# P times V of a sliding-window attention in eight 64x32 array tiles, with the halves added on GpSimd and the transposed maxima four slots later

## The chip, the core and the metric

The kernel runs on one core of a Trainium2 chip. A core has five engines with a queue each, which take their instructions in order and meet through semaphores: TensorE (PE in the profile, its weight loads PEld), VectorE (DVE), ScalarE (ACT), GpSimd (POOL) and SyncE (SP), which here only issues DMAs. TensorE multiplies out of SBUF into PSUM, which has eight banks of 128 partitions by 512 fp32 values. The metric is the device time of one execution in microseconds (us).

## The reference

The output is x + attention(LN(x)) + GEGLU(LN(x)) for 2048 tokens of width 640, all in fp32. What the change touches is the attention: 32 heads of width 20, each query seeing itself and the 255 keys before it.

```python
B, S, D = x.shape                       # 1, 2048, 640
H = 32; Dh = D // H; W = 256
qkv = (x @ wqkv) ...                    # q, k, v: heads of width 20
scores = jnp.einsum("bhqd,bhkd->bhqk", q, k) * (Dh ** -0.5)
mask = (idx[:, None] - idx[None, :] >= 0) & (idx[:, None] - idx[None, :] < W)
p = _softmax(jnp.where(mask, scores, -1e9), axis=-1)
o = jnp.einsum("bhqk,bhkd->bhqd", p, v)
# o @ wo is added to x and to (gelu(xn @ w_gate) * (xn @ w_up)) @ w_down
```

## The kernel before

The attention is cut into 32 units, one for each group `g` of four heads and each chunk `c` of 512 queries (`u = 4 * g + c`). It is run between about 90 and 575 us of the span in an order written out by hand: a loop over units, each of 14 slots, that says in every slot which instructions each engine gets next. Into each slot it also puts some 2.4 dense matmuls (128x512) of other work, the q, k and v projections and the first gate and up tiles, so that TensorE always has something to do (`pull_fill`, line 110).

A unit passes through these steps, the first two of them ahead of its own slots.

- `max_pair` (line 522): bf16 scores of 64 queries by up to 320 keys for the row maxima, in 64x64 tiles of the array, two PSUM banks for a pair. VectorE reduces each bank with a mask (line 526, into `junk` and `mx`). Two pairs are issued as a burst at slots 0, 4 and 8, and at slot 0 two more behind the P times V product. The order behind that product is: four banks of maxima, then the first score of the next unit.
- `max_end` (lines 543 to 546): the negated maxima `nm` are transposed by TensorE into `ps_n`, copied by ScalarE to `mr` and sent by a DMA from ScalarE's queue into two extra rows of the query stack `qs`, so that the score matmul subtracts the maximum. `MXD` sets how many slots after the last maxima this happens: 6, which is slot 6, eight slots ahead of the unit's first score.
- `exp_piece` (lines 581 and 583): for s = 0 to 11 a bank of scores, transposed (keys in the partitions), then exp on ScalarE into a tile `P`. Four of them, one for each head, share a `P` tile; three `P` tiles X, Z and Y (s = 0 to 3, 4 to 7, 8 to 11) hold the unit's key blocks. s = 0 is in slot 0, 1 to 4 in slot 2, 5 and 6 in slot 4, 7 and 8 in slot 8, 9 to 11 in slot 10.
- `clear` (lines 594 and 597): GpSimd zeroes, one slot after the last exp of a `P` tile, what lies outside the window, 128 keys by 128 queries of four heads at a time. For Y those are three instructions, the last of them for key block b+3.
- `av_unit` (lines 608 and 612): at slot 0 of the next unit, V (128 keys by 20 columns and a column of ones, 32 columns of the array for each head) times P. Four heads run beside each other in four 128x32 tiles, six key blocks one after the other in the order X, Z, Y, 1536 columns in all (four blocks and 1152 columns for c = 0). All goes into one bank `ps_o`; ScalarE copies it to `ob`, and SyncE stores it three slots later.

The banks `ps_m`, `ps_n`, `ps_e` and `ps_o` come out of one pool of six (`psr`, tag `ring`); the other two hold the dense tiles. A tile of the pool may be written once its last reader is done, and TensorE, which takes its queue in order, waits at the first matmul into it.

```python
BURSTS = 0, 4, 8
SCORES = {0: range(0, 1), 2: range(1, 5), 4: range(5, 7), 8: range(7, 9), 10: range(9, 12)}
MXD = 6
psr = pp.enter_context(tc.tile_pool(name="psr", bufs=6, space=PSUM, reuse_waits="tile"))
```

Of the kernel before, what the change touches and what calls it, by code (L numbers as in the profile page):

```python
# [9 lines left out]
F32 = mybir.dt.float32  # L10
F32R = mybir.dt.float32r
BF = mybir.dt.bfloat16
AF = mybir.ActivationFunctionType
OP = mybir.AluOpType
# [5 lines left out]
C = 512  # L20
# [15 lines left out]
VEARLY = 2  # L36
VLEAD = 40
POOL_SLOTS = 13, 0, 1, 2, 3, 4, 5, 6, 7
MXD = 6
KSLOT = 9  # L40
LAG = 3, 5, 4, 4, 4, 4, 3, 3, 4, 3, 2, 1, 1, 1
NFA = 4
# [28 lines left out]
def block_kernel(ctx, tc, x, wqk, wv, wgu, wdo, wdl, out):  # L71
    nc = tc.nc
# [120 lines left out]
    done = set()  # L193
    now = [None]

    def at(slot, fn, *a):
        acts.setdefault(slot, []).append((fn, a))
# [31 lines left out]
    def defer(n, fn, *a):  # L229
        if now[0] is None:  # L230
            fn(*a)
        else:
            at(now[0] + n, fn, *a)
# [190 lines left out]
    with tc.tile_pool(name="lp", bufs=1, side="right") as lp:  # L424
# [5 lines left out]
        ps = psd.tile([128, C], F32, name="ps_u", tag="dn")  # L430
# [48 lines left out]
    vtiles = dict(enumerate(v0[2]))  # L479
    pf.close()  # L480
    psr = pp.enter_context(tc.tile_pool(name="psr", bufs=6, space=PSUM, reuse_waits="tile"))
    ap = pr.enter_context(tc.tile_pool(name="ap", bufs=2, side="right", reuse_waits="tile"))
# [14 lines left out]
    def bank(name):  # L497
        return psr.tile([128, C], F32, name=name, tag="ring")
# [49 lines left out]
    def pieces(c):  # L548
        b = 4 * c
        X = [(b, 0, 0, 384)] + ([(b - 2, 384, 0, 128)] if c else [])  # L550
        Y = [(b + 1, 0, 128, 384), (b + 3, 384, 384, 128)]
        Z = ([(b - 1, 0, 0, 256)] if c else []) + [(b + 2, 256, 256, 256)]
        return X, Z, Y
# [11 lines left out]
    pts = {}  # L565
# [21 lines left out]
    def clear(u, bi):  # L587
        c = u % NC
        pt = pts[u, bi]
        for p in pieces(c)[bi]:  # L590
            for col, diag in diag_tail(*p, c):
# [4 lines left out]
                else:  # L596
                    nc.gpsimd.affine_select(out=a, in_=a, pattern=[[0, 4], [-1, 128]], compare_op=OP.is_ge,  # L597
                                            fill=0.0, base=-1, channel_multiplier=1)

    def av_unit(u):  # L600
        g, c = divmod(u, NC)
        o, v = bank("ps_o"), vtiles[g]
        todo = [(pts[u, bi], *p) for bi, ps in enumerate(pieces(c)) for p in ps]
        for i, (pt, kb, col, q0, n) in enumerate(todo):
            assert (id(v), kb) in done, (u, kb)
            for j in range(4):
                w0_ = kb * 84 + 21 * j
                nc.tensor.matmul(o[32 * j:32 * j + 32, q0:q0 + n], v[:, w0_:w0_ + 32], pt[:, j, col:col + n],  # L608
                                 start=i == 0, stop=i == len(todo) - 1, skip_group_check=True,
                                 tile_position=(0, 32 * j))  # L610
        ob = ap.tile([128, C], F32, name="ob", tag="ob", bufs=1)
        nc.scalar.activation(ob, o, AF.Copy)  # L612

        def store():
            for j in range(4):
                nc.sync.dma_start(od[c].rearrange("(d h) t -> h d t", h=H)[4 * g + j], ob[32 * j:32 * j + DH, :])
            nc.sync.dma_start(sd[c][4 * g:4 * g + 4, :], ob[DH::32, :])

        defer(3, store)

    def load_gu(f):
        raws = []
# [163 lines left out]
    def pull_max(n, slot):  # L786
        for _ in range(n):
# [4 lines left out]
            if x[1] == 7:  # L792
                at(slot + (MXD if slot >= 0 else 4), max_end, x[0])

# [9 lines left out]
    def attention():  # L804
# [18 lines left out]
        for u in range(NU + 1):  # L823
            for i in range(NS):
                T = now[0] = NS * u + i
                for fn, a in tick():
                    fn(*a)
                if i in BURSTS:
                    pull_max(2, T)
                if i == 0 and u:  # L830
                    av_unit(u - 1)
                    flush()
                    pull_max(2, T)
                for s in SCORES.get(i, ()) if u < NU else ():
# [673 lines left out]
```

## Time and profile before

| what | value |
|---|---|
| time, median of 3 runs | 1047.59 us (1047.58 to 1047.95) |
| span of the profiled execution | 1046.8 us, about 0.8 us less than the median of the runs |
| granted TensorE clock, mean | 0.999 |
| TensorE matmul busy | 1035.2 us, 99% of the span |
| VectorE, ScalarE, GpSimd busy | 70%, 49%, 32% of the span |
| P times V (line 608) | 1408 matmul records, 84.3 us busy |
| copy of it (line 612) | 32, 597 ns each |

An fp32 matmul of the program stands in the trace as two weight loads and two matmul records. Records carry modelled ends that reach past the start of the next matmul, so what a group costs TensorE is read from its start to the start of what follows. Times in the rows are from the span's start; `[0.33 <-ACT ob L612]` is idle time before the row and what ended it.

### The profile page before, as it was taken

How to read it: one execution, taken by the hardware profiler on the slowest of the kernel's cores; microseconds unless marked ns; L12 is line 12 of the kernel's file. 1: busy time of each engine (PE TensorE's matmuls, PEld its weight loads, DVE VectorE, ACT ScalarE, POOL GpSimd, SP SyncE). 2: the span in 40 equal slices, each digit the busy share in tenths (PEclk: the TensorE clock that was granted, in tenths of full speed). 3: DMA queues.
4: the chain of work that ended last, by engine and by line, in shares of the span. 5: the costliest groups of instructions: out<-in, count | busy, mean ns of one | idle time of the engine just before them, and what ended most of it. 6: DMA issues, size and time to landing. Idle time of an engine off the chain costs nothing.

```text
span 1046.8 us, 22733 instructions
## 1 busy us (share of the span) xinstructions
PE 1035.2 (99%) x7997; PEld 827.6 (79%) x7997; DVE 730.8 (70%) x2007; ACT 513.5 (49%) x1088; POOL 333.8 (32%) x503
## 2 busy tenths in 40 slices
PE   8999999999999999999999999999999999999998
PEld 7987666666677766666666888888888999999998
DVE  8745656666665556677662677877655889888887
ACT  4444666765665566656565532223324554333332
POOL 5122667766464458474635111110110000000000
PEclk9999999999999999999999999999999999999999
DMA  5651465545332344444322557677217874443342
GB/s 200 189 150 59 135 183 159 179 148 180 96 117 72 111 145 144 139 130 130 112 79 75 191 189 244 213 251 253 100 61 250 270 241 137 134 128 113 125 134 94
DMA packets 105179, 158.56 MB, mean 151 GB/s; under 512 B 15420, under 2 KB 60092, under 8 KB 105064
## 3 DMA queue, kind: packets, MB, share of 16 engines
q1 hardware_dynamic: 102680, 150.95, 45.0%
q10 hardware_dynamic: 2384, 6.16, 1.9%
q8 instruction: 63, 1.03, 0.4%
q14 instruction: 52, 0.43, 0.1%
HBM read 101.78 MB, written 54.92 MB: 150 GB/s over the span
## 4 chain that ended last, share of the span: by engine, by line
PE 92%; DVE 3%; DMA 2%; ACT 1%; POOL 1%; issue 1%; SPq 0%; DVEq 0%; POOLq 0%; ACTq 0%
PE ps_g L952 21%; PE ps L1219 21%; PE ps_d L110 21%; PE ps_e L581 8%; PE ps_o L608 7%; PE ps_v L110 7%; PE ps_m L522 4%; PE ps_g L110 1%; PE ps_t L181 1%; DVE junk L526 1%; DMA qs<-qd 1%; PE ps_d L356 1%; DVE ss L1057 0%; POOL pt L259 0%; DVE at L1057 0%
## 5 line engine op out<-in xcount | busy, mean ns | idle before, releaser
L526 DVE CUSTOM_DVE_ANT_0 junk<-ps_m,mask 128x320 bf16<-128x320 f32 (+2 forms) x512 | 243.2, 475 | 144.5 <-PE ps_m L522 85.5
L583 ACT ACTIVATE P<-ps_e 128x512 f32<-128x512 f32 (+2 forms) x384 | 195.6, 578 | 60.9 <-PE ps_e L581 59.0
L1219 PE MATMUL ps<-wb,at 128*128 128x320 f32 x999 | 156.0, 309 | 0.0
L1219 PEld LDWEIGHTS ps<-wb,at 128*128 128x128 f32 x999 | 148.9, 188 | 0.3
L594 POOL TENSOR_SCALAR_AFFINE_SELECT P<-P 128x512 f32<-128x512 f32 x128 | 83.9, 657 | 141.0 <-ACT P L583 138.3
L581 PE MATMUL ps_e<-qs,ks 124*128 124x128 bf16 (+2 forms) x704 | 108.0, 277 | 0.7 <-DVE mx L526 0.4
L110 PE MATMUL ps_d<-xh,wqh 128*128 128x512 f32 x350 | 104.4, 410 | 0.0
L110 PE MATMUL ps_d<-xl,wqh 128*128 128x512 f32 x350 | 104.2, 409 | 0.0
L110 PE MATMUL ps_d<-xh,wql 128*128 128x512 f32 x350 | 103.8, 409 | 0.0
L1219 PE MATMUL ps<-wt,at 128*128 128x320 f32 x552 | 89.2, 309 | 0.4 <-DVE u L1057 0.4
L581 PEld LDWEIGHTS <-ks 124*128 124x128 bf16 x704 | 50.8, 98 | 47.8 <-issue 30.1
L608 PE MATMUL ps_o<-P,v 128*32 128x384 f32 (+2 forms) x1408 | 84.3, 386 | 0.6 <-DVE mx L526 0.6
L1219 PEld LDWEIGHTS ps<-wt,at 128*128 128x128 f32 x552 | 82.9, 188 | 0.9 <-DVE u L1057 0.9
L597 POOL TENSOR_SCALAR_AFFINE_SELECT P<-P 128x512 f32<-128x512 f32 x112 | 70.8, 643 | 33.7 <-ACT P L583 33.7
L1173 ACT ACTIVATE at<-ss 128x512 fp32r<-128x512 f32 x59 | 37.3, 632 | 89.6 <-DVE ss L1057 89.6
L103 POOL TENSOR_TENSOR wql<-wr,wqh 128x640 fp32r<-128x640 f32 x11 | 17.6, 1607 | 174.0 <-PE ps_g L952 129.4
L110 PEld LDWEIGHTS ps_d<-xh,wql 128*128 128x128 f32 x350 | 63.9, 189 | 11.1 <-issue 0.3
L608 PEld LDWEIGHTS ps_o<-P,v 128*32 128x32 f32 x1408 | 41.5, 110 | 39.0 <-issue 21.1
L110 PEld LDWEIGHTS ps_d<-xl,wqh 128*128 128x128 f32 x350 | 63.8, 189 | 10.5 <-issue 0.2
L110 PEld LDWEIGHTS ps_d<-xh,wqh 128*128 128x128 f32 x350 | 63.4, 189 | 10.7 <-issue 0.3
L259 POOL TENSOR_TENSOR pt<-r,pt 128x512 bf16<-128x512 f32 x40 | 46.8, 1170 | 67.3 <-ACT pt L258 67.2
L612 ACT ACTIVATE ob<-ps_o 128x512 f32<-128x512 f32 x32 | 19.1, 597 | 86.6 <-PE ps_o L608 72.3
(194 smaller groups left out, 1846.0 us busy)
## 6 DMA issues: line engine op xcount, KB each, us to landing
hr<-hd SPq DMA_DIRECT2D x104, 128.0 KB
hd<-he SPq DMA_DIRECT2D x50, 256.0 KB
wr<-wgu SPq DMA_DIRECT2D x27, 320.0 KB
qs<-qd SPq DMA_DIRECT2D x64, 120.0 KB
ks<-kd SPq DMA_DIRECT2D x64, 120.0 KB
xi<-x SPq DMA_DIRECT2D x16, 320.0 KB
qs<-qd SPq DMA_DIRECT2D x64, 80.0 KB
ks<-kd SPq DMA_DIRECT2D x64, 80.0 KB
```

The costliest lines, as they stand in the source:

```text
L110: nc.tensor.matmul(ps, a(k), b(k), start=n == 0, stop=n == 3 * nk - 1)
L259: nc.gpsimd.tensor_tensor(out=pt[:, l, :], in0=r, in1=pt[:, 1, :], op=OP.subtract)
L522: nc.tensor.matmul(ps[64 * h:64 * h + 64, lo:hi], q[rows, j, q0:q0 + 64], keys, start=True, stop=True, tile_position=(64 * r, 64 * h))
L526: nc.vector.tensor_tensor_reduce(out=junk[:, 0:n], in0=ps[:, 0:n], in1=mask[:, 320 - n:320], scale=1.0, scalar=NEG, op0=OP.add, op1=OP.max ...
L581: nc.tensor.matmul(ps[:, col:col + n], k[0:QROWS, j, kc:kc + 128], q[0:QROWS, j, q0:q0 + n], start=True, stop=True)
L583: nc.scalar.activation(pt[:, j, lo:hi], ps[:, lo:hi], AF.Exp, scale=SCALE)
L594: nc.gpsimd.affine_select(out=a, in_=a, pattern=[[0, 4], [1, 128]], compare_op=OP.is_ge, fill=0.0, base=0, channel_multiplier=-1)
L597: nc.gpsimd.affine_select(out=a, in_=a, pattern=[[0, 4], [-1, 128]], compare_op=OP.is_ge, fill=0.0, base=-1, channel_multiplier=1)
L608: nc.tensor.matmul(o[32 * j:32 * j + 32, q0:q0 + n], v[:, w0_:w0_ + 32], pt[:, j, col:col + n], start=i == 0, stop=i == len(todo) - 1, ski ...
L952: nc.tensor.matmul(ps, i, j, start=first and n == 0, stop=n == len(work) - 1, skip_group_check=True)
L1173: nc.scalar.activation(hi[:, 3:7], s, AF.Copy)
L1219: nc.tensor.matmul(ps[bank][:, 0:HD], *work[bank][j], start=bank not in begun, stop=final[p, bank] == n and j == len(work[bank]) - 1, skip ...
```

## The change

It has three parts.

1. The product is split by keys: each block of 128 keys becomes two halves of 64, which use the upper and the lower 64 rows of the array, so that eight 64x32 tiles (two halves by four heads) take part. Each half of a block meets only the queries of its own window, at most 320 columns (384 where c = 0 and the first key block fills the columns ahead of it). Halves of equal width are paired, in a new order: for c > 0 first key block b+0 with itself, then half 0 of b+3 with half 1 of b-2, and so on, with b+1 last. Each half has a bank of its own, so a unit takes two banks `ps_o` instead of one.
2. ScalarE copies both banks, the second into the first quarter of the unit's `P` tile Y (`other`), and one slot later GpSimd adds the two (new line 630). The store comes a slot later, in the fourth.
3. `MXD` is 10: the transpose of the negated maxima stands at the head of slot 10, ahead of the scores s = 9 to 11, and its DMA behind their exps.

```diff
-MXD = 6
+MXD = 10
...
+    def windows(c):
+        r = {}
+        for bi, ps in enumerate(pieces(c)):
+            for kb, col, q0, n in ps:
+                for h in range(2):
+                    first = 128 * (kb - 4 * c) + 64 * h
+                    lo = max(0, first) if kb else 0
+                    hi = min(C, first + 320)
+                    r[h, kb - 4 * c] = bi, kb, col + lo - q0, lo, hi - lo
+        pairs = [((0, 0), (1, 0)), ((0, 3), (1, -2)), ((0, -2), (1, 3)), ((0, 2), (1, -1)), ((0, -1), (1, 2)),
+                 ((0, 1), (1, 1))]
+        if not c:
+            pairs = [((0, d), (1, d)) for d in range(4)]
+        return [[(h, *r[h, d]) for h, d in p] for p in pairs]
...
-        o, v = bank("ps_o"), vtiles[g]
-        todo = [(pts[u, bi], *p) for bi, ps in enumerate(pieces(c)) for p in ps]
...
+        halves, v = [bank("ps_o") for _ in range(2)], vtiles[g]
+        todo = windows(c)
+        for i, pair in enumerate(todo):
             for j in range(4):
...
+                for h, bi, kb, col, q0, n in pair:
+                    rows, w0_ = slice(64 * h, 64 * h + 64), kb * 84 + 21 * j
+                    nc.tensor.matmul(halves[h][32 * j:32 * j + 32, q0:q0 + n], v[rows, w0_:w0_ + 32],
+                                     pts[u, bi][rows, j, col:col + n], start=i == 0, stop=i == len(todo) - 1,
+                                     skip_group_check=True, tile_position=(64 * h, 32 * j))
+        ob, other = ap.tile([128, C], F32, name="ob", tag="ob", bufs=1), pts[u, 2][:, 0, :]
+        nc.scalar.activation(ob, halves[0], AF.Copy)
+        nc.scalar.activation(other, halves[1], AF.Copy)
+        defer(1, lambda: nc.gpsimd.tensor_tensor(out=ob, in0=ob, in1=other, op=OP.add))
...
-        defer(3, store)
+        defer(4, store)
```

How the instructions stand is shown at three places, all of the unit u = 10 (c = 2); a name in brackets says whose semaphore an instruction waits for. The first is TensorE's product, before: X (384 and 128 columns), Z (twice 256), Y (384 and 128), each with its own wait for GpSimd's clears.

```order
L608 MATMUL ps_o<-P,v 32x384 [waits Activation_49,Pool_49]
L608 MATMUL ps_o<-P,v 32x384 x3
L608 MATMUL ps_o<-P,v 32x128 [waits Pool_49]
L608 MATMUL ps_o<-P,v 32x128 x3
L608 MATMUL ps_o<-P,v 32x256 [waits Pool_49]
L608 MATMUL ps_o<-P,v 32x256 x3
L608 MATMUL ps_o<-P,v 32x256 [waits Pool_49]
L608 MATMUL ps_o<-P,v 32x256 x3
L608 MATMUL ps_o<-P,v 32x384 [waits Pool_49]
L608 MATMUL ps_o<-P,v 32x384 x2
L608 MATMUL ps_o<-P,v 32x384 [waits Activation_49]
L608 MATMUL ps_o<-P,v 32x128 [waits Pool_49]
```

The same product with the change (line 624), eight matmuls for each pair of halves:

```order
L624 MATMUL ps_o<-P,v 32x320 [waits Activation_49,Pool_49]
L624 MATMUL ps_o<-P,v 32x320 [waits Activation_49]
L624 MATMUL ps_o<-P,v 32x320 x6
L624 MATMUL ps_o<-P,v 32x128 [waits Pool_49]
L624 MATMUL ps_o<-P,v 32x128 x7
L624 MATMUL ps_o<-P,v 32x64 x8
L624 MATMUL ps_o<-P,v 32x256 x8
L624 MATMUL ps_o<-P,v 32x192 x8
L624 MATMUL ps_o<-P,v 32x320 x8
```

The last wait for GpSimd, for key block b+3 out of Y, has moved from behind five blocks to behind the first pair.

The second place is on TensorE too: the end of the burst behind the product and the next unit's first score (`ps_e`, line 581), before,

```order
L522 LDWEIGHTS qs_166
L522 MATMUL ps_m<-ks_169,qs_166 64x320
L581 LDWEIGHTS ks_171 [waits DMAHW6_49]
L581 MATMUL ps_e<-qs_168,ks_171 128x128 [waits DVE_49]
L581 LDWEIGHTS ks_172
L581 MATMUL ps_e<-qs_168,ks_172 128x384
L110 MATMUL ps_d<-xh_77,wql 128x512
```

and with the change:

```order
L522 LDWEIGHTS qs_166
L522 MATMUL ps_m<-ks_169,qs_166 64x320
L581 LDWEIGHTS ks_171 [waits DMAHW3_49,DMAHW0_49]
L581 MATMUL ps_e<-qs_168,ks_171 128x128 [waits Activation_49]
L581 LDWEIGHTS ks_172
L581 MATMUL ps_e<-qs_168,ks_172 128x384
L110 MATMUL ps_d<-xh_77,wql 128x512
```

The first score's bank is freed by a reduction of VectorE before and by ScalarE with the change: in the built program it is the bank of the product's first half, in 29 of the 30 units that have a second burst (in the other, u = 9, the burst's last bank is that one).

The third place is ScalarE's queue from slot 8 to the copy of the next product, before,

```order
L545 ACTIVATE mr<-ps_n 32x128 [waits PE_49]
L546 DMA qs_168<-mr 2x16x128 [waits DMAHW6_49,Activation_49]
L583 ACTIVATE P<-ps_e 128x512 [waits PE_49]
L583 ACTIVATE P<-ps_e 128x512 [waits PE_49,Pool_49]
L665 ACTIVATE he<-he 128x512 [waits DVE_49]
L583 ACTIVATE P<-ps_e 128x512 [waits PE_49] x3
L612 ACTIVATE ob<-ps_o 128x512 [waits DMAHW2_49,DMAHW5_49,DMAHW1_49,DMAHW7_49,DMAHW0_49,PE_49]
```

and with the change:

```order
L583 ACTIVATE P<-ps_e 128x512 [waits PE_49]
L583 ACTIVATE P<-ps_e 128x512 [waits PE_49,Pool_49]
L683 ACTIVATE he<-he 128x512 [waits DVE_49]
L545 ACTIVATE mr<-ps_n 32x128 [waits PE_49]
L583 ACTIVATE P<-ps_e 128x512 [waits PE_49] x3
L546 DMA qs_168<-mr 2x16x128 [waits DMAHW3_49,Activation_49]
L628 ACTIVATE ob<-ps_o 128x512 [waits DMAHW5_49,DMAHW6_49,DMAHW1_49,DMAHW7_49,DMAHW0_49,PE_49]
L629 ACTIVATE P<-ps_o 128x512 [waits PE_49,Pool_49]
```

The copy `mr` stands ahead of the three exps of slot 10 and its DMA behind them, and a second copy follows the first.

More of the change, by code (lines that the diff above doesn't have):

```diff
@@ L600, in av_unit @@
     def av_unit(u):
         g, c = divmod(u, NC)
-        o, v = bank("ps_o"), vtiles[g]
-        todo = [(pts[u, bi], *p) for bi, ps in enumerate(pieces(c)) for p in ps]
-        for i, (pt, kb, col, q0, n) in enumerate(todo):
-            assert (id(v), kb) in done, (u, kb)
+        halves, v = [bank("ps_o") for _ in range(2)], vtiles[g]
+        todo = windows(c)
+        for i, pair in enumerate(todo):
             for j in range(4):
[L607 to L610, printed above, removed]
@@ L611, in av_unit @@
-        ob = ap.tile([128, C], F32, name="ob", tag="ob", bufs=1)
-        nc.scalar.activation(ob, o, AF.Copy)
+                for h, bi, kb, col, q0, n in pair:
+                    assert (id(v), kb) in done, (u, kb)
+                    rows, w0_ = slice(64 * h, 64 * h + 64), kb * 84 + 21 * j
+                    nc.tensor.matmul(halves[h][32 * j:32 * j + 32, q0:q0 + n], v[rows, w0_:w0_ + 32],
+                                     pts[u, bi][rows, j, col:col + n], start=i == 0, stop=i == len(todo) - 1,
+                                     skip_group_check=True, tile_position=(64 * h, 32 * j))
```

## The prediction

> **What bounds the kernel now.** I read the page first, then one row of busy times for the attention, then TensorE's order of time around two products.
>
> ```profile
> span 1046.8 us, 22733 instructions
> PE 1035.2 (99%) x7997; PEld 827.6 (79%) x7997; DVE 730.8 (70%) x2007; ACT 513.5 (49%) x1088; POOL 333.8 (32%) x503
> PE 92%; DVE 3%; DMA 2%; ACT 1%; POOL 1%; issue 1%; SPq 0%; DVEq 0%; POOLq 0%; ACTq 0%
> ...
> 90.00:575.00 485.00, 481.67 (x4756) 323.20 (x4745) 302.30 (x1120) 299.16 (x652) 280.55 (x440) 1.00 0.42 127
> ```
>
> TensorE carries 92% of the chain that ended last, and in the attention (90 to 575 us; the columns are length, then PE, PEld, DVE, ACT and POOL busy, clock, DMA share and GB/s) it has matmuls for 481.67 of 485.00 us, at full clock. The other engines are busy some 60%. So whatever shortens or stalls TensorE there moves the end one for one, and a wait of another engine costs nothing until TensorE meets it.
>
> ```profile
> 165.97 2.15 PE L608 MATMUL ps_o<-P,v 128*32 128x384 f32 x32
> 168.04 0.47 PE L522 MATMUL ps_m<-ks,qs 60*64 60x320 bf16 x8
> ...
> 240.89 2.80 PE L608 MATMUL ps_o<-P,v 128*32 128x384 f32 x48
> 243.62 0.46 PE L522 MATMUL ps_m<-ks,qs 60*64 60x320 bf16 x5
> 244.41 0.33 PE L522 MATMUL ps_m<-ks,qs 60*64 60x320 bf16 x3 [0.33 <-ACT ob L612]
> 244.67 0.39 PE L581 MATMUL ps_e<-qs,ks 124*128 124x128 bf16 x2
> ...
> 256.51 0.36 PE L522 MATMUL ps_m<-ks,qs 60*64 60x64 bf16 x12
> 256.81 2.80 PE L608 MATMUL ps_o<-P,v 128*32 128x384 f32 x48
> 259.53 0.47 PE L522 MATMUL ps_m<-ks,qs 60*64 60x320 bf16 x8
> 259.93 0.39 PE L581 MATMUL ps_e<-qs,ks 124*128 124x128 bf16 x2
> ...
> 261.08 1.05 PE L581 MATMUL ps_e<-qs,ks 124*128 124x128 bf16 x8
> ```
>
> These are three products (starts are the first column) with the burst and the first score behind them. From start to start a product costs 256.81 to 259.53 = 2.72 us, or 2.07 for c = 0 (165.97 to 168.04). At 240.89 the burst stops halfway for the copy `ob`: that will be the model for the change.
>
> **The product.** The two lengths differ by 384 columns and 0.65 us, so a column costs 1.69 ns and 2.72 - 1536 x 1.69 ns leaves 0.12 us for start and drain. If all eight tiles run at once, a unit has 1280 columns instead of 1536: 256 x 1.69 ns = 0.43 us less. For c = 0 the longer half has 1024 instead of 1152: 0.22 us less. Sum: 24 x 0.433 + 8 x 0.217 = 12.1 us gained. Do the two row halves run at once? No fp32 row shows it, but the maxima do so in bf16: their eight matmuls of 320 columns in four 64x64 tiles take 0.40 us (259.53 to 259.93), 0.05 each, drain included, where the dense stage pays 0.156 for one of 320:
>
> ```profile
> L1219 PE MATMUL ps<-wb,at 128*128 128x320 f32 x999 | 156.0, 309 | 0.0
> ...
> 256.81 0.53 PE L608 MATMUL ps_o<-P,v 128*32 128x384 f32 x4
> ```
>
> The second row, asked for the 50 ns up to 256.84, shows four fp32 column tiles started within 0.03 us. I take the full 12.1; the other end, halves in turn, is a rival.
>
> **The first score's wait.** The product's two banks leave four of the six for the bursts, and the first score takes the first half's bank, which the first copy has to empty.
>
> ```profile
> 243.76 0.60 ACT L612 ACTIVATE ob<-ps_o 128x512 f32<-128x512 f32 x1 [1.46 <-PE ps_o L608]
> ...
> 259.67 0.60 ACT L612 ACTIVATE ob<-ps_o 128x512 f32<-128x512 f32 x1 [4.20 <-PE ps_o L608]
> ...
> L522 PE MATMUL ps_m<-ks,qs 60*64 60x320 bf16 x512 | 30.5, 308 | 0.7 <-ACT ob L612 0.7
> ```
>
> ScalarE stands idle when the product ends, so the copy starts 0.14 us behind it (259.67 - 259.53), takes 0.60, and TensorE resumes 0.05 later (243.76 + 0.60 to 244.41): 0.79 us behind the product, where the score now comes at 0.40 (259.93). That is +0.39 us for a unit. The last row holds before's whole price for it: two units whose burst meets that bank, 0.33 idle each, and whose score comes 1.05 us behind the product (244.67 - 243.62). In one of the two it will be 0.79; in another one the burst's last bank is still the product's, so 1.05 stays. Sum: 28 x 0.39 - 0.26 = 10.7 us lost. The second copy costs TensorE nothing: it ends 0.14 + 2 x 0.60 = 1.34 us behind the product at the latest, and its bank is next used in slot 2, which begins 1.15 us behind the first score (259.93 to 261.08), so at 1.94. So nearly all of the product's gain goes back here. In the Trainium skill, "TensorEngine Tiling (Array Packing)", section Performance Considerations, PSUM Bottleneck, says that tiling speeds up TensorE but not the emptying of PSUM, so that the copy can become the bottleneck; the wait at 244.41 agrees.
>
> **The clears.** For c > 0 the second pair needs the last clear of Y; before, Y came behind X and Z. The first pair ends 0.02 + 320 x 1.69 ns = 0.56 us into the product. To see what GpSimd still has to do then, I asked for the work on `P` from 0.51 us (0.05 for the semaphore, as above) to 2.60 us into each of the 24 products:
>
> ```profile
> 119.96:122.05 2.09, 2.09 (x47) 1.13 (x36) 0.00 (x0) 0.00 (x0) 1.00 0.61 199
> 135.00:137.09 2.09, 2.09 (x47) 1.08 (x36) 0.00 (x0) 1.69 (x3) 1.00 0.78 243
> ...
> 568.50:570.59 2.09, 2.09 (x47) 1.13 (x36) 0.00 (x0) 0.73 (x2) 1.00 0.05 22
> sum 50.18, PE 50.18 PEld 27.04 ACT 0.00 POOL 9.38; mean PE 2.09 PEld 1.13 ACT 0.00 POOL 0.39
> ```
>
> The fourth busy time is POOL: nothing in the first stretch, 1.69 us in the worst, 9.38 in all (the first two, the last, and the sum of the 24). The clears run back to back there, so this is what TensorE would wait: 9.4 us lost, ahead of the copy, so it adds to the wait above. For c = 0 the second pair needs only earlier clears, and I put it at nothing.
>
> **The add.** GpSimd gets 32 additions of 128x512 fp32, which no row shows. The nearest are
>
> ```profile
> L259 POOL TENSOR_TENSOR pt<-r,pt 128x512 bf16<-128x512 f32 x40 | 46.8, 1170 | 67.3 <-ACT pt L258 67.2 <-DMA ks<-kd 0.2
> L739 POOL TENSOR_TENSOR tx<-tx,xl 128x256 f32<-128x256 f32 x48 | 36.2, 754 | 1.7
> ...
> 182.00:194.00 12.00, 11.20 (x18) 1.00 0.57 173
> 391.60:403.00 11.40, 11.12 (x18) 1.00 0.36 112
> ```
>
> so 1.17 to 1.51 us (twice 0.754). Behind it on the queue stand the clears. In most units GpSimd idles for microseconds before these; in the two stretches shown (POOL busy is the number behind the length) only 0.80 and 0.28 us are left, so 1.5 us more delays the clears by 0.7 and 1.2. I take 1.9 us lost, between nothing and 7.5 (five such units, 1.5 each). The store, one slot later behind the add, is followed by SyncE's other transfers, which are needed a unit later: nothing.
>
> **The moved transpose.** The matmul is the same, and its bank is free earlier than the scores'. ScalarE gets `mr` (0.26) ahead of three exps and 0.62 us of DMA issue behind them:
>
> ```profile
> 250.10 0.23 PE L543 MATMUL ps_n<-identb,nm 128*128 128x128 bf16 x1
> ...
> 250.84 0.26 ACT L545 ACTIVATE mr<-ps_n 32x128 bf16<-32x128 f32 x1
> 251.13 0.65 ACTq L546 DMA_DIRECT2D qs<-mr  x1
> ...
> 253.90 1.57 ACT L583 ACTIVATE P<-ps_e 128x512 f32<-128x512 f32 x3
> ```
>
> Here the exps would end at 255.47 and the issue at 256.12; the score that reads the row came at 259.93 and would come no more than 0.43 sooner: 3.4 us for a transfer of 8 KB. Nothing, with that as cover.
>
> **Sum.** -12.1 + 10.7 + 9.4 + 1.9 = +9.9 us on the execution's 1046.8, and 0.8 more to the median: 1057.5 us, 0.9% slower.
>
> **Rivals.**
> - The clears don't bind, because GpSimd comes earlier in the new order: -12.1 + 10.7 = -1.4, 1046.2 us, no change. Against it: nothing that feeds the clears is moved ahead.
> - Faster: the first score waits for an older reader of ScalarE's and not for the copy. Then the score comes at 0.40 again, before's two long waits go too (-1.3), and the sum is -12.1 - 1.3 + 9.4 + 1.9 = -2.1, or -4.0 if the add hides: 1044.5. It decides from a wait under 0.2 us on. Against it: the bank is the first half's.
> - The short matmuls are bound by their starts. Twelve of the maxima take 0.30 us (256.51 to 256.81), 25 ns each; 96 records at 25 ns and 0.12 make a product 2.52 us, which gains 0.20 instead of 0.43 in 24 units: 5.6 us more than my sum, 1063. Against it: the four starts within 0.03 us. The Trainium skill, "TensorE: Matmul & The Clock Gate", Part 1 (Wait — 56ns, not 53.3ns?), has this as a rule, no start closer than about 25 ns to the last; the four starts disagree.
> - The halves take turns in fp32: 2560 columns, 24 x 1.73 + 8 x 1.41 = 53 us lost instead of 12 gained; Y then waits less, some 2.5: 53 + 10.7 + 2.5, 1114 us.
> - The maxima come late: a landing 1 us past the 3.4 would cost 31 units 1 us each, 1088.
>
> **How the numbers follow.** What a measurement can tell from no change is about 0.2%, 2.1 us. The forecast has 0.66, with a range of its own of 1051 to 1062 (the add's two ends, and the waits a quarter off); clears that don't bind 0.07 (same); the older reader 0.06 and both together 0.04 (faster, 1034 to 1045); bound starts 0.07, halves in turn 0.06, late maxima 0.04 (all slower). So faster 0.10, same 0.07, slower 0.83. The range takes in forecast, bound starts and the clears' case, 0.80: 1046 to 1064.
>
> **What would show it.** In the profile after, a product with no wait for GpSimd in it costs 2.29 us (c > 0); line 581 or 522 idles behind ACT's copy of `ps_o` in every unit but two, with the score 0.79 us behind the product; and line 624 idles behind POOL at the second pair, 0.2 us in many units and over 1 in a few. A product of 4.4 us would show halves in turn, 2.5 bound starts, and a wait for a DMA at line 581 late maxima. The forecast is wrong if GpSimd's clears move against the product, since the 9.4 us come from their place in the trace of before.

## The result, and the profile after

The changed kernel takes 1063.95 us (median; 1063.40 to 1064.86), the kernel before beside it 1047.77 us: 1.0152 times as long, with a 95% interval of 1.0138 to 1.0167. It is slower, by 16 us. The profiled execution has a span of 1062.1 us, 15.3 more than before.

From the profile after: the page's span, busy times and chain of waits, then the row of busy times for the attention (90 to 586 us; length, then PE, PEld, DVE, ACT and POOL busy, clock, DMA share, GB/s).

```profile
span 1062.1 us, 25620 instructions
PE 1035.2 (97%) x9405; PEld 842.0 (79%) x9405; DVE 738.5 (70%) x2007; ACT 526.9 (50%) x1120; POOL 373.6 (35%) x535
PE 78%; DVE 6%; ACT 5%; POOL 4%; DMA 4%; issue 2%; SPq 1%; DVEq 0%; ACTq 0%; POOLq 0%
...
90.00:586.00 496.00, 476.71 (x6147) 333.63 (x6135) 305.94 (x1115) 311.78 (x681) 317.69 (x470) 1.00 0.42 124
```

TensorE is busy for the same 1035.2 us as before; by the page the whole difference is time in which it has nothing running. (Busy time counts the records' modelled ends, which reach into the waits; by starts the products did get 7.5 us shorter, as the table below shows.) Its share of the chain fell from 92% to 78%, and the rest went to ScalarE, GpSimd, VectorE and DMA. The clock is full in both.

Next the groups of lines 581 (scores) and 624 (the product, line 608 before), and TensorE's order of time: an undisturbed product (unit 21; units count the products from 0), the worst one (unit 2), and the last.

```profile
L581 PE MATMUL ps_e<-qs,ks 124*128 124x128 bf16 (+2 forms) x704 | 107.1, 276 | 7.8 <-ACT ob L628 6.1 <-DVE mx L526 1.5
L624 PE MATMUL ps_o<-P,v 64*32 64x320 f32 (+5 forms) x2816 | 81.8, 351 | 7.4 <-POOL P L594 5.8 <-POOL P L597 1.1 <-DVE mx L526 0.4
```

```profile
135.81 0.77 PE L624 MATMUL ps_o<-P,v 64*32 64x320 f32 x16
138.15 2.01 PE L624 MATMUL ps_o<-P,v 64*32 64x128 f32 x80 [1.57 <-POOL P L594]
140.09 0.47 PE L522 MATMUL ps_m<-ks,qs 60*64 60x320 bf16 x8
140.83 0.38 PE L581 MATMUL ps_e<-qs,ks 124*128 124x128 bf16 x2 [0.27 <-ACT ob L628]
...
429.20 2.55 PE L624 MATMUL ps_o<-P,v 64*32 64x320 f32 x96
431.69 0.47 PE L522 MATMUL ps_m<-ks,qs 60*64 60x320 bf16 x8
432.42 0.38 PE L581 MATMUL ps_e<-qs,ks 124*128 124x128 bf16 x2 [0.27 <-ACT ob L628]
...
583.02 2.01 PE L624 MATMUL ps_o<-P,v 64*32 64x128 f32 x80 [0.53 <-POOL P L594]
584.97 0.73 PE L110 MATMUL ps_d<-xl,wqh 128*128 128x512 f32 x2
586.19 0.96 PE L110 MATMUL ps_g<-xh,wqh 128*128 128x512 f32 x3 [0.49 <-ACT P L629]
```

Three things are to be seen. A product that waits for nothing takes 2.48 us (429.20 to 431.69), where it took 2.73. Behind it the first score waits for ScalarE's copy of the first half, 0.74 us behind the product instead of 0.40. And at unit 2 the second pair of 128 columns waits for GpSimd's clears: the product takes 4.28 us. The last row is new too: the dense stage behind the last product stops for the second copy.

I split the execution at three starts in each unit: the product's first record, the burst's first record behind it, and the first score. Summed over the units, against before:

| stretch | change, us |
|---|---|
| before the first product | +0.6 |
| products, without waits for GpSimd (24 x 0.245 and 8 x 0.197 shorter) | -7.5 |
| waits for GpSimd inside products, c > 0 | +9.9 |
| the same, c = 0 (units 0 and 24) | +2.1 |
| product to first score | +9.9 |
| first score to next product | -0.8 |
| behind the last product | about +1.1 |
| span | +15.3 |

A wait for GpSimd is what a product lasts over 2.48 us (c > 0) or 1.88 us (c = 0). It is more than the 7.4 us of idle time at line 624, because the modelled end of the matmul before covers the first 0.2 to 0.3 us of each wait (at unit 2 the row shows 1.57 us, and by starts it is 1.80).

### The profile page after: what moved, and what is told of

It reads as the page before. It is cut to its first block, busy times and chain, and to the rows that moved or that the text cites. A ratio compares the mean times of both kernels' runs of the same rounds, so it can differ in the third digit from the quotient of the medians.

```text
span 1062.1 us, 25620 instructions
## 1 busy us (share of the span) xinstructions
PE 1035.2 (97%) x9405; PEld 842.0 (79%) x9405; DVE 738.5 (70%) x2007; ACT 526.9 (50%) x1120; POOL 373.6 (35%) x535
## 4 chain that ended last, share of the span: by engine, by line
PE 78%; DVE 6%; ACT 5%; POOL 4%; DMA 4%; issue 2%; SPq 1%; DVEq 0%; ACTq 0%; POOLq 0%
PE ps_g L970 20%; PE ps L1237 18%; PE ps_d L110 17%; PE ps_e L581 6%; PE ps_v L110 6%; PE ps_o L624 6%; PE ps_m L522 3%; DVE junk L526 2%; ACT P L583 2%; POOL P L594 2%; PE ps_g L110 1%; POOL P L597 1%; ACT ob L628 1%; PE ps_t L181 1%; DVE at L1075 1%
## 5 line engine op out<-in xcount | busy, mean ns | idle before, releaser
L624 PE MATMUL ps_o<-P,v 64*32 64x320 f32 (+5 forms) x2816 | 81.8, 351 | 7.4 <-POOL P L594 5.8
L581 PEld LDWEIGHTS <-ks 124*128 124x128 bf16 x704 | 53.3, 98 | 44.9 <-issue 27.4
L110 PEld LDWEIGHTS ps_d<-xh,wqh 128*128 128x128 f32 x350 | 63.8, 189 | 11.4 <-issue 0.3
L624 PEld LDWEIGHTS ps_o<-P,v 64*32 64x32 f32 x2816 | 49.7, 105 | 27.6 <-POOL P L594 18.4
L522 PEld LDWEIGHTS <-qs 60*64 60x64 bf16 x1472 | 27.2, 105 | 51.0 <-issue 44.3
```

The lines of the kernel that those rows point to most:

```text
L110: nc.tensor.matmul(ps, a(k), b(k), start=n == 0, stop=n == 3 * nk - 1)
L522: nc.tensor.matmul(ps[64 * h:64 * h + 64, lo:hi], q[rows, j, q0:q0 + 64], keys, start=True, stop=True, tile_position=(64 * r, 64 * h))
L581: nc.tensor.matmul(ps[:, col:col + n], k[0:QROWS, j, kc:kc + 128], q[0:QROWS, j, q0:q0 + n], start=True, stop=True)
L624: nc.tensor.matmul(halves[h][32 * j:32 * j + 32, q0:q0 + n], v[rows, w0_:w0_ + 32], pts[u, bi][rows, j, col:col + n], start=i == 0, stop=i ...
```

## The experiments

Each is compared with the kernel before, run on the same chip; 1.0152 is the changed kernel's ratio. Differences between experiments are taken between these ratios, or between starts in the traces.

**Two banks for the product.** First I wanted the bank alone, without tiles:

```diff
-        o, v = bank("ps_o"), vtiles[g]
+        o, spare, v = bank("ps_o"), bank("ps_o"), vtiles[g]
```

> The kernel before, whose product now takes two banks of the ring and leaves the second one empty; nothing else differs. Theory (the first score waits because its bank is one further on in the ring, and that is the bank the copy empties): the score comes 0.74 us behind the product, as in the changed kernel, and not 0.40, in some 28 units: 28 x 0.34 - 0.3 = +9.2 us, 1057 us. Rival (the wait belongs to the two copies, or to the tiles, and not to the number of banks): the score stays at 0.40 and the time at 1047.7.

Measured: 1.0001 (0.9992 to 1.0011), and nothing in the trace moved: the score stayed at 0.40, and the same two bursts as before stopped for the copy. A tile that nothing writes evidently held no bank, so this run tells nothing about the theory. The next one fills both banks:

```diff
-        o, v = bank("ps_o"), vtiles[g]
+        halves, v = [bank("ps_o") for _ in range(2)], vtiles[g]
...
+                o = halves[int(n == 256)]
...
-        nc.scalar.activation(ob, o, AF.Copy)
+        ob, other = ap.tile([128, C], F32, name="ob", tag="ob", bufs=1), pts[u, 2][:, 0, :]
+        a = 0 if c else 256
+        nc.scalar.activation(ob, halves[0], AF.Copy)
+        nc.scalar.activation(other[:, a:C], halves[1][:, a:C], AF.Copy)
+        defer(1, lambda: nc.gpsimd.tensor_tensor(out=ob[:, a:C], in0=ob[:, a:C], in1=other[:, a:C], op=OP.add))
...
```

> The kernel before, its product still of whole blocks of 128 rows in four tiles and in the old order, but written into two banks (the pieces X and Y into one, Z into the other), both copied by ScalarE and added on GpSimd. So the changed kernel without its tiles, its order of pairs and its moved transpose. Theory (the bank is what the first score waits for): the product stays at 2.73 us, the score comes 0.74 to 0.79 us behind it and the rest of the unit gives 0.09 of that back, as in the changed kernel: 30 x 0.25 = 7.5, with 1.5 at the first and the last unit 9 us over before, 1057 us. Rival (the score's wait comes of the shorter product and its tiles): 1048 to 1050 us, the score at 0.40.

Measured: 1.0119 (1.0104 to 1.0134), 12.4 us slower. TensorE at unit 21 of this kernel, and its line of scores:

```profile
428.26 2.80 PE L609 MATMUL ps_o<-P,v 128*32 128x384 f32 x48
430.99 0.47 PE L522 MATMUL ps_m<-ks,qs 60*64 60x320 bf16 x8
431.77 0.38 PE L581 MATMUL ps_e<-qs,ks 124*128 124x128 bf16 x2 [0.32 <-ACT ob L614]
...
L581 PE MATMUL ps_e<-qs,ks 124*128 124x128 bf16 (+2 forms) x704 | 107.6, 277 | 8.3 <-ACT ob L614 6.1 <-DMA qs<-qd 0.8 <-DVE mx L526 0.4
```

The product is the old one, 2.73 us, and the score comes 0.78 to 0.79 us behind it (1.27 in the two units that had 1.05). The stretches between product and score grew by 11.3 us in all, and the rest of the units gave only 0.6 back. Another 0.8 us is a wait of unit 24's product for GpSimd, and 0.9 stand behind the last product. So the price of the second bank is paid without any tile. The theory holds, and its price of 9 us was low: this rest gives back next to nothing, where I had put 0.09 a unit.

**The first score one slot later.**

```diff
-SCORES = {0: range(0, 1), 2: range(1, 5), 4: range(5, 7), 8: range(7, 9), 10: range(9, 12)}
+SCORES = {1: range(0, 1), 2: range(1, 5), 4: range(5, 7), 8: range(7, 9), 10: range(9, 12)}
```

> The changed kernel with the unit's first score one slot later, so that two to four dense matmuls stand between the burst and this score. Theory: they cover the copy that empties the score's bank; the 9.9 us between products and first scores come back, 1064.0 - 9.9 = 1054 us, and line 581 has no idle time behind ScalarE's copy. Rival (the wait only moves: the scores of slot 2 or the exponentials behind them come as late as they did): 1064 us, with the idle time behind ScalarE at another line.

Measured: 1.0127 (1.0112 to 1.0142), 2.6 us below the changed kernel and not 9.9. TensorE at unit 21, and at a product with c = 0 (unit 28, at 538.72); then the kernel's longest kinds of wait (total, times, longest):

```profile
432.69 0.47 PE L522 MATMUL ps_m<-ks,qs 60*64 60x320 bf16 x8
433.09 0.96 PE L110 MATMUL ps_d<-xh,wqh 128*128 128x512 f32 x3
433.89 0.40 PE L581 MATMUL ps_e<-qs,ks 124*128 124x128 bf16 x2
...
538.72 1.95 PE L624 MATMUL ps_o<-P,v 64*32 64x320 f32 x64
540.60 0.91 PE L522 MATMUL ps_m<-ks,qs 60*64 60x320 bf16 x8
541.44 0.96 PE L110 MATMUL ps_d<-xh,wqh 128*128 128x512 f32 x3
...
PE ps_o L624 <- POOL P L594: 6.5, 10, 1.6
PE ps_t L181 <- DVE xi L164: 2.4, 3, 1.5
PE ps_m L522 <- DMA qs<-qd: 2.2, 3, 1.5
```

The wait for the copy is gone: in an ordinary c > 0 unit the stretch from product to next product is 0.07 us over before where the changed kernel has 0.25 (medians), so nearly 0.2 us did come back in each of 16 such units, 3.3 us together. I had expected the 0.34 at the score; the changed kernel's unit had already given 0.09 of it back, in dense work that came closer. It went again elsewhere: the wait for `qs` near 160 us grew (the rest of unit 3 is 1.4 us longer than in the changed kernel), GpSimd's clears came 0.6 us later against unit 6's product, and with c = 0 nothing was won, since there the burst itself takes 0.84 us (540.60 to 541.44) instead of 0.40, ahead of the score. That happens only behind the c = 0 product of 1.88 us in two banks; that VectorE has not yet emptied the banks of the burst before is what I take for its cause. Its rows fit (the last of those four reductions runs from 540.63 to 541.12 us), but no run here isolates it. In the profiled execution the units as a whole gave nothing back, 0.3 us more than in the changed kernel; its span is 0.8 us shorter, and that came behind the last product. So both expectations were partly wrong.

**Y's pairs last.**

```diff
-        pairs = [((0, 0), (1, 0)), ((0, 3), (1, -2)), ((0, -2), (1, 3)), ((0, 2), (1, -1)), ((0, -1), (1, 2)),
-                 ((0, 1), (1, 1))]
+        pairs = [((0, 0), (1, 0)), ((0, 2), (1, -1)), ((0, -1), (1, 2)), ((0, 1), (1, 1)), ((0, 3), (1, -2)),
+                 ((0, -2), (1, 3))]
         if not c:
-            pairs = [((0, d), (1, d)) for d in range(4)]
+            pairs = [((0, d), (1, d)) for d in (0, 2, 1, 3)]
```

> The changed kernel with the three pairs that need Y (the clears' last piece) put behind the three that do not; for c = 0 the order is 0, 2, 1, 3. Y is then needed 768 columns, 1.3 us, into the product and not 0.56. Theory (the waits for GpSimd inside the products are Y's clears alone): each wait of a c > 0 unit shrinks by up to 0.75 us, from 9.9 us in all to 1.6, and those for c = 0 from 2.1 to 1.2: 1064.0 - 9.2 = 1054.8 us; a product that waits for nothing stays at 2.48 us, since the short pairs are only moved. Rival (GpSimd is behind with X and Z too, because of the additions): the waits move to the second pair as it now is, and the time stays near 1064.

Measured: 1.0056 (1.0039 to 1.0073), 1054.14 us. The group of the product, then unit 21 and the longest wait behind unit 3:

```profile
L624 PE MATMUL ps_o<-P,v 64*32 64x320 f32 (+5 forms) x2816 | 75.7, 349 | 1.1 <-POOL P L597 0.7 <-DVE mx L526 0.4
...
159.10 0.19 PE L522 MATMUL ps_m<-ks,qs 60*64 60x64 bf16 x1 [1.54 <-DMA qs<-qd]
...
426.72 2.45 PE L624 MATMUL ps_o<-P,v 64*32 64x320 f32 x96
429.10 0.47 PE L522 MATMUL ps_m<-ks,qs 60*64 60x320 bf16 x8
429.88 0.38 PE L581 MATMUL ps_e<-qs,ks 124*128 124x128 bf16 x2 [0.31 <-ACT ob L628]
```

The clears hardly wait any more: 0.5 us in the c > 0 units, 1.6 in the two with c = 0. The time came out as expected, but from three terms and not one. The waits gave 9.9 (12.0 to 2.1). The undisturbed product went from 2.48 to 2.376 us, 2.6 us in 24 units, which I had not expected. And 4.4 us went again behind the products: 0.9 at the first scores and 3.5 in the rest of the units, 2.1 of it in unit 3, where a load of `qs` near 159 us did not come earlier for a kernel that had reached this place 1.7 us sooner.

**Why the undisturbed product got shorter.** These are the starts of the 64-column pair's matmul records and of those behind it, unit 21, in ns behind the product's start, from both traces (each pair is two passes of eight tiles; at 0.84 ns a column, half of the 1.69 for both passes, a pass of 64 columns lasts 54 ns):

```
changed kernel, third pair:
  64 columns   781 789 795 802 812 824 837 841 | 844 852 858 869 885 902 919 935
  256 columns  893 976 993 1009 1026 1043 1059 1076 | 1112 ...
Y last, 64 columns as the last pair:
  128 columns  1857 1864 1871 1878 1884 1890 1897 1904 | 1966 1973 1980 1987 1993 2000 2006 2013
  64 columns   2075 2082 2090 2096 2102 2119 2131 2135 | 2138 2146 2152 2163 2180 2196 2213 2230
```

With Y last the eight tiles start within 47 ns in every pass up to the 64-column pair, 6.6 apart. In that pair the starts spread to 16.6 ns, and in the middle of the product the tiles then stay out of step: the next pass starts over 183 ns, and the last pass of the whole product still over 202 ns (1922 to 2124). At the end of the product there is nothing left to put out of step. The weight loads of the short pair stand 16.6 ns apart too (with Y last two rows of them, 2048 to 2148 and 2077 to 2176), and its last five matmuls each start 53 or 54 ns behind one. So the rate of weight loads may be what holds the short starts; no run isolates it. Two runs put this to the test. One moves the 64-column pair alone:

```diff
-        pairs = [((0, 0), (1, 0)), ((0, 3), (1, -2)), ((0, -2), (1, 3)), ((0, 2), (1, -1)), ((0, -1), (1, 2)),
-                 ((0, 1), (1, 1))]
+        pairs = [((0, 0), (1, 0)), ((0, 3), (1, -2)), ((0, 2), (1, -1)), ((0, -1), (1, 2)), ((0, 1), (1, 1)),
+                 ((0, -2), (1, 3))]
```

> The changed kernel with one pair moved: the one of 64 columns goes from third place to the last; the second pair still needs Y. Theory (in the middle of the product the 64-column pair puts the eight tiles out of step, and they stay so): an undisturbed product costs 2.38 us, as with Y last, and not 2.48; the waits for GpSimd stay at 12: 24 x 0.108 = 2.6 us less, 1061.4 us. Rival (the 0.1 us came of Y's late place, or of the two short pairs standing together): 2.48 us and 1064.

Measured: 1.0136 (1.0113 to 1.0159), 1061.85 us.

```profile
428.25 2.45 PE L624 MATMUL ps_o<-P,v 64*32 64x320 f32 x96
430.63 0.47 PE L522 MATMUL ps_m<-ks,qs 60*64 60x320 bf16 x8
...
L624 PE MATMUL ps_o<-P,v 64*32 64x320 f32 (+5 forms) x2816 | 78.4, 349 | 7.7 <-POOL P L594 6.0 <-POOL P L597 1.1 <-DVE mx L526 0.4
```

2.376 us again, with the waits for GpSimd nearly unchanged (11.4 us for 12.0). So it is the place of the 64-column pair, and neither Y nor the neighbouring 128-column pair. Two things fit less well. The 128-column pair, still second, puts the tiles out of step too: from the 256-column pair on the starts go to 16.6 ns apart, over 92 ns, and stay so. But the product is as short as with Y last; a spread of 92 ns is not yet a loss, the 202 ns behind a 64-column pair is. And the kernel as a whole gained some 1.7 us and not 2.6, a difference that the intervals do not resolve: by starts the products give 3.2 us with their waits, and 1.7 go again at the first scores, which come 0.83 us behind most products and not 0.74. The other run lets the heads do their short pairs at different times (with Y last):

```diff
+TAILS = (0, 1, 2), (0, 2, 1), (1, 2, 0), (2, 1, 0)
...
+            seq, t = (todo[:3] + [todo[3 + k] for k in TAILS[j]] if c else todo), 0
+            for i, pair in enumerate(seq):
+                plan.append((t, i, j, pair, i == len(seq) - 1))
+                t += max(p[5] for p in pair)
+        for _, i, j, pair, last in sorted(plan, key=lambda p: p[:3]):
```

> As the run with Y last, and the four heads take the three last pairs (320, 128 and 64 columns) in four different orders, the matmuls written in the order in which their columns come up; same matmuls, same number of starts. Theory (the product costs 2.48 us and not 2.29 because all eight tiles do their shortest matmuls together, and starts are then 16.6 ns apart): at most four short ones now come together, and a product costs 2.29 to 2.35 us: 24 x 0.13 to 24 x 0.19 = 3 to 4.6 us below the run with Y last, 1050 to 1052 us if that gives 1054.8. Rival (96 starts at about 25 ns bound the product, whatever the order): 2.48 us and the same time as the run with Y last.

Measured: 1.0081 (1.0066 to 1.0096), 1056.37 us, 2.6 us over the run with Y last.

```profile
428.46 2.60 PE L630 MATMUL ps_o<-P,v 64*32 64x320 f32 x96
430.99 0.47 PE L523 MATMUL ps_m<-ks,qs 60*64 60x320 bf16 x8
```

The product takes 2.53 us, longer than with all heads in step. I had this wrong: mixed lengths do not spread the cost, they make it worse. In the trace the last pairs of the four heads (starts from 1.32 us on) fall out of step the same way as behind the 64-column pair. A reading that fits all three orders is that TensorE takes the matmuls in the order written, and one whose tile is still at work holds those behind it; it is not shown, and the weight loads are another. Unequal lengths need not cost much either: with c = 0 the two halves have different lengths (384 and 320 columns in the first pair, 128 and 64 in the last), the starts of a pass spread over up to 154 ns, and the product takes 1.88 us where the longer half's 1024 columns alone make 1.85 by the prediction's 1.69 ns. That the rival's bound of 25 ns a start does not hold is shown by the 6.6 ns; and 25 ns each, close to 2.376 us for 96 starts, does not give the 2.48 and 2.53 us that the same 96 starts take in other orders.

**The moved transpose, undone.**

```diff
-MXD = 10
+MXD = 6
```

> The changed kernel with the transpose of the maxima back in its old place (MXD = 6). Theory (the move costs and brings nothing): 1063 to 1065 us. Rival A (the later maxima are awaited somewhere): 1061 or less. Rival B (the move made room for the copies on ScalarE): 1066 or more.

Measured: 1.0146 (1.0131 to 1.0161), the same as the changed kernel, as far as these intervals can tell (some 1.5 us each way). So in sum the move costs and brings nothing. Within the unit it does: from product to next product an ordinary c > 0 unit is 0.31 us over before with the transpose in its old place and 0.25 with it moved (medians), and what the move saves there is lost mostly in units 3 and 9, which take 1.1 and 1.2 us longer with it between product and next product.

**The addition left out.**

```diff
-        defer(1, lambda: nc.gpsimd.tensor_tensor(out=ob, in0=ob, in1=other, op=OP.add))
```

> The changed kernel without the addition on GpSimd, so that the second half's sums are left out of the output; the copies stay. Theory (the clears are late by themselves, the addition's backlog is 1.9 us of it): the waits for GpSimd in the products fall from 12.0 to about 10 us, 1062 us. Rival (the additions push the clears back in most of the units that wait): the waits fall to 3 to 5 us, 1055 to 1057 us.

Measured: 1.0123 (1.0106 to 1.0139), 3 us below the changed kernel. The product's group here, and unit 24 (c = 0) first in the changed kernel and then here:

```profile
475.62 0.88 PE L624 MATMUL ps_o<-P,v 64*32 64x320 f32 x16
477.63 1.42 PE L624 MATMUL ps_o<-P,v 64*32 64x320 f32 x48 [1.14 <-POOL P L597]
```

```profile
L624 PE MATMUL ps_o<-P,v 64*32 64x320 f32 (+5 forms) x2816 | 81.6, 351 | 6.6 <-POOL P L594 6.0 <-DVE mx L526 0.4
...
474.13 1.95 PE L624 MATMUL ps_o<-P,v 64*32 64x320 f32 x64
476.01 0.91 PE L522 MATMUL ps_m<-ks,qs 60*64 60x320 bf16 x8
```

The waits in the c > 0 products are 10.3 us without the addition and 9.9 with it: the clears that bind there are late by themselves. What the addition costs is one wait of 1.5 us, at unit 24, and some 1.9 us in the stretches between score and next product, 1.0 of it in unit 3, where a load of `qs` is awaited. This last part is not sure to be the addition's: two executions that have the same instructions up to there, of the last two runs below, differ by 1.2 us in the same stretch.

**A kernel without the known losses.** Y last, the first score in slot 1, and the old product where c = 0 (`av_whole` is `av_unit` of before: 128 rows, one bank, one copy):

```diff
+        if not c:
+            return av_whole(u, g, c)
```

> The changed kernel with Y's pairs last, the first score in slot 1, and for c = 0 the product of before (128 rows, one bank, one copy, no addition). Theory: 24 products of 2.376 us save 24 x 0.35 = 8.4; the score in slot 1 leaves 0.05 us of the wait in 24 units, 1.2; the first unit, the last copy and the wait for qs near 160 us cost 1 to 4: 1048.2 - 8.4 + 1.2 + 2.5 = 1043.5 us, between 1042 and 1046. Rival (a score in slot 1 costs the unit what it saves, as the run with this alone seemed to say): 1048 to 1051 us.

Measured: 1.0046 (1.0029 to 1.0063), 1052.81 us: 9 us too high, and slower than before. TensorE's longest kind of wait (total, times, longest), and three of its places:

```profile
PE ps_m L522 <- DMA qs<-qd: 5.4, 6, 1.2
...
143.27 0.47 PE L522 MATMUL ps_m<-ks,qs 60*64 60x64 bf16 x15 [0.87 <-DMA qs<-qd]
159.08 0.19 PE L522 MATMUL ps_m<-ks,qs 60*64 60x64 bf16 x1 [1.16 <-DMA qs<-qd]
160.21 0.47 PE L522 MATMUL ps_m<-ks,qs 60*64 60x64 bf16 x15 [0.94 <-DMA qs<-qd]
```

An undisturbed c > 0 unit now gains as worked out, 0.35 in the product less 0.06 behind it. But the kernel is 4.2 us behind before at unit 10, above all for these loads, and loses 1.2 more at unit 24 to GpSimd. Is the addition the cause? It was put on VectorE, from the bank:

```diff
-        nc.scalar.activation(other, halves[1], AF.Copy)
-        defer(1, lambda: nc.gpsimd.tensor_tensor(out=ob, in0=ob, in1=other, op=OP.add))
+        defer(1, lambda: nc.vector.tensor_tensor(out=ob, in0=ob, in1=halves[1], op=OP.add))
```

> The run with Y last, the score in slot 1 and the old product for c = 0, and the second half added by VectorE straight from its bank onto the copied first half; ScalarE's second copy and GpSimd's addition go. Theory (what that run still lost against before came of the addition on GpSimd: one wait of 1.2 us at the twenty-fifth product, and the stack of keys and queries, whose GpSimd steps stand behind it and whose loads TensorE waited 5.4 us for before 165 us): some 4 us less than its 1052.8, 1047 to 1050 us. Rival A (those loads are late because TensorE is early, and 0.7 us more for VectorE in a unit delays the maxima): 1052 us or more. Rival B (all of it hides, and the 0.29 us saved in each c > 0 unit is left): 1044 us or less.

Measured: 1.0054 (1.0036 to 1.0072), 1054.43 us, no better, and the time of rival A. The run is not a clean test, since the addition on VectorE has a price of its own: an ordinary unit gives 0.1 us less between product and next product than in the run before (medians 0.21 and 0.09 over before), some 2.6 us in 24, and TensorE three times waits for it. GpSimd ahead of unit 24, in this kernel:

```profile
459.47 0.73 POOL L775 TENSOR_TENSOR tx<-tx,xl 128x256 f32<-128x256 f32 x1
465.92 0.74 POOL L775 TENSOR_TENSOR tx<-xh 128x256 f32<-128x256 f32 x1 [5.72 <-DMA td<-tx]
466.61 0.64 POOL L594 TENSOR_SCALAR_AFFINE_SELECT P<-P 128x512 f32<-128x512 f32 x1
```

The wait at unit 24 grew to 2.1 us though no addition stands on GpSimd: its queue stops 5.72 us for the transfer of `td` from the tile that it fills next, and the clears stand behind that. A wait for `qs` near 160 us stayed too (1.3 us), though all such waits fell from 5.4 to 3.6 us. So neither is the addition's alone; for unit 24 it is one of the things that shift GpSimd's queue against that transfer. The last two runs use the tiled product only from u = 10 on (`TILED` is 10), the second not at u = 23, with the transpose in its old place:

```diff
+    def tiled(u):
+        return u >= TILED and u % NC > 0
...
+    def scores(u, i):
+        if i < 2:
+            return range(0, 1) if i == tiled(u - 1) else ()
+        return SCORES.get(i, ())
```

> The kernel before up to the tenth product (u = 0 to 9, transpose in its old place); from u = 10 on the 17 products with c > 0 are the tiled ones with Y last, their second half added on GpSimd, and the first score behind each of them in slot 1. Theory (an undisturbed unit gains 0.35 in the product and loses 0.06 behind it, and what the run with the old product for c = 0 lost came before the tenth product, of loads of qs that do not come earlier, and once at the twenty-fifth product): 17 x 0.29 = 4.9 less, 1.2 lost at the twenty-fifth product and 0.5 at the last copy: 1048.4 - 3.2 = 1045.2 us, between 1044 and 1047. Rival (the waits for loads and for GpSimd only come at other units): 1048 to 1051 us.

> As the run with the late units, but the twenty-fourth product (u = 23) is the old one, so that no addition stands on GpSimd ahead of the clears that the twenty-fifth product awaits. Theory: 16 x 0.29 = 4.6 less and 0.5 at the last copy, 1044.3 us. Rival (that wait is of GpSimd's wait for the transfer of td, addition or not): 1045.5 us, as the other.

Measured: 1.0001 (0.9992 to 1.0010) and 0.9998 (0.9990 to 1.0007), both the same as before. Unit 24 waits 1.1 us in the first and for nothing in the second. Two things kept the gain away. The tiled units gained less than in the run with the old product for c = 0: 0.2 us in the median and not 0.29, which fits the 0.06 us more that the transpose in its old place costs; and the products of units 10 and 26 are 0.34 us longer, as all tiles but the first start 0.36 us late. From unit 10 to 29 they gave 1.9 and 1.7 us where 0.29 each makes 4.4 and 4.1. And of the 1.0 and 1.1 us gained up to unit 20, two thirds are lost at one place, the end of a burst 6 us behind the start of unit 20's product; the rows are from before, from the first and from the second of these runs, and from the run with the empty second bank, which has the instructions of before:

```profile
412.29 0.47 PE L522 MATMUL ps_m<-ks,qs 60*64 60x64 bf16 x15 [0.69 <-DVE r L273]
```

```profile
412.55 0.47 PE L523 MATMUL ps_m<-ks,qs 60*64 60x64 bf16 x15 [1.28 <-DMA qs<-qd]
```

```profile
410.97 0.19 PE L523 MATMUL ps_m<-ks,qs 60*64 60x64 bf16 x1 [0.43 <-DVE r L274]
412.15 0.47 PE L523 MATMUL ps_m<-ks,qs 60*64 60x64 bf16 x15 [0.99 <-DMA qs<-qd]
```

```profile
411.78 0.47 PE L522 MATMUL ps_m<-ks,qs 60*64 60x64 bf16 x16
```

In the first three the burst goes on at 412.2 to 412.6 us, and the runs that arrive earlier wait longer, for the load of `qs`. (Before's row names VectorE's `r`, but that ends at 411.63; that this wait too is for `qs` is my reading.) A product that is faster there only meets the stack of queries sooner. But the load has no fixed time: in the fourth row, the burst passes at 411.78 without a stop. So executions of the same instructions differ here by nearly as much as the tiled units had gained, and how much of the loss is of coming early, and how much of that, stays open. No version that I ran is faster than the kernel before.

## Why the prediction was right, and where it was not

The forecast of slower held, for the reasons given: the second bank and the clears take back more than the product saves. The size did not. The forecast's own case went from 1051 to 1062 us, and 1063.95 lies outside it; it lies within 1046 to 1064 only because the range took in the rival of bound starts, whose mechanism is not the one that came. That is luck. By its own steps:

- **The product** (-12.1): the step that failed, a term too large by 4.6 us. It says that all columns cost 1.69 ns when eight tiles run at once. With c = 0, where the windows are long, it held (1.88 us for 1.85). With c > 0 the product took 2.48 instead of 2.29 us, and the term is -7.5. Of the 0.19 us, 0.11 is the 64-column pair putting the tiles out of step in the middle, which the runs with that pair last took away; some 0.09 stays even then. These 4.6 us are nearly all of the 5.4 by which the span missed the sum of 9.9. The rival of bound starts named 2.52 us and 1063, and its sign, a product of 2.5 us, is what the trace shows; but the 6.6 ns exclude its mechanism, and what is held are the starts of short pairs. By what, weight loads or the order of the matmuls, is open.
- **The first score's wait** (+10.7): right. It measured 9.9, with 0.74 us behind the product instead of 0.79, and the run with two banks and the old product has 0.785 and 11.3 us. That c = 0 units come at 0.84, through a longer burst, was not foreseen.
- **The clears' wait** (+9.4): right, 9.9 us, with 1.8 in the worst unit, the one that the rows of before named; putting Y last took nearly all of it away.
- **The add** (+1.9): wrong in its mechanism, and near in size, 3 us by the run without it, by luck. The additions do not push the c > 0 clears back (10.3 us of waits without them). c = 0, put at nothing, holds the 1.5 us of unit 24, and perhaps the 1.0 us of unit 3's wait for `qs`.
- **The moved transpose** (0): right in sum, though not for every unit.
- **Not in the sum**: about 1.1 us behind the last product, where the next stage waits for the second copy, 0.6 before the first, and 0.8 given back in the units.

With the measured terms the sum is -7.5 + 9.9 + 9.9 + 2.1 - 0.8 + 1.7 = +15.3, the span's difference.

## What to carry to other kernels

Splitting a product into smaller tiles buys columns, but what it costs lies around it: the second bank moves the wait of whoever takes the next bank (here 0.39 us a unit, alone enough to undo the gain), and a new order of the pieces can ask for the latest piece first. Put the shortest matmuls of concurrent tiles at the end of the product (2.376 us here, 2.48 with them in the middle), and give concurrent tiles their lengths in the same order (mixed they took 2.53). And a gain in a stage counts only as far as the loads that feed it have slack: here kernels that came sooner to a load of `qs` waited longer for it, though executions of one kernel differ there as well.

## What the hardware showed that I had not expected

- In eight 64x32 fp32 tiles in step, starts of different tiles are 6.6 ns apart in passes of 128 to 320 columns (the run with Y last), and up to 16.6 ns apart in a pass of 64 columns (54 ns). Behind a 64-column pair in the middle of a product the tiles stay out of step to its end, over up to 202 ns, and the product takes 0.11 us more; behind a 128-column pair in the middle they do so over 92 ns, and it takes no more. The Trainium skill, "TensorE: Matmul & The Clock Gate", Part 1 (Wait — 56ns, not 53.3ns?), lets no start come closer than about 25 ns to the last; these starts, in different tiles, do not agree.
- In one case tiles that do matmuls of different lengths at the same time lost time against tiles in step: 2.53 us instead of 2.376 for the same matmuls.
- An addition of 128x512 fp32 on GpSimd takes 1.29 us in the trace (1.27 to 1.30), between the 1.17 and 1.51 us of the forecast.
